# Attention and a gated FFN in one kernel: 128-query scores from halves of q and k, and the second pass's low halves of weights on VectorE

## The chip, the cores and the metric

The kernel runs on one core of one Trainium2 chip. The metric is the device time of one execution in microseconds. The kernel before takes 665.92 us, the median of three runs (665.81 to 666.36).

## The reference

Causal attention with 4 batches, 12 heads, 448 positions and a head size of 64, then an RMS norm over the 768 model columns and a gated FFN with 1536 hidden columns on all 1792 tokens, in fp32:

```python
scores = scale * np.matmul(q, k.transpose(0, 1, 3, 2))
scores = np.where(mask, -1000000000.0, scores)
scores = scores - np.max(scores, axis=-1, keepdims=True)
attn = np.exp(scores)
attn = attn / (np.sum(attn, axis=-1, keepdims=True) + 1e-09)
x = np.matmul(attn, v)            # then (tokens, 768)
rms = np.sqrt(np.mean(x * x, axis=-1, keepdims=True) + 1e-06)
xn = x / rms * rms_g
g = xn @ w_gate
silu = g * (1.0 / (1.0 + np.exp(-g)))
val = xn @ w_val
return silu * val @ w_out
```

## The kernel before

The tokens are cut into three groups. Groups 0 and 1 hold the first 256 queries of two batches each, group 2 the last 192 queries of all four. Attention is cut into 60 units; a unit is a pair of heads (64 rows of the array each) and a set of queries. Units 0 to 11 make group 0, 12 to 23 group 1 (256 queries each). Units 24 to 59 make group 2: in each six, four of 128 queries of one batch (kind 1) and two of 64 queries of two batches (kind 2). In order of their numbers, 24, 25 and 26 are kind 1, 27 and 28 kind 2, 29 to 32 kind 1, 33 and 34 kind 2, and so on.

The FFN multiplies in fp32r. Each operand is cut into a high half (`h`, a cast on ScalarE) and a low half (`l`, what is left, a subtraction on VectorE or GpSimd), and a product is three: high by high, high by low, low by high (L508 to L510 in the first two passes, L658 in the third). The scores (L195) are plain fp32 products of the loaded q and k, which hold both in one tile (`qk_r`): 128 columns of queries and 384 of keys for kind 1.

Three passes run over the FFN. While the first works on group 0, group 1's attention is made; while the second works on group 1, that of group 2. The third, for group 2, follows alone. In a pass a tick is two row blocks of one weight unit, six products of 128x512, then a step of the attention if one is due. Delayed work is posted to a later tick (`post`), and a table of delays (`T`) says how many ticks later; `tick()` then emits it at the end of that tick. The order on every engine is the order in which the code emits it.

In the second pass the attention goes in visits of two units, one visit about every four ticks (`round_of_two`). The visit of p makes the scores of units p + 3 and p + 4 and the products with v of p and p + 1. The scores stay in PSUM until VectorE masks them (L204), ScalarE takes the exponential (L207), VectorE the reciprocal of the sums (L216) and GpSimd multiplies by it (L212). In the next three ticks and at the start of the next visit the weights are transposed, one head a tick, into the single bank t (L251), which VectorE (L255) or ScalarE (L257) copies out.

The q and k of unit p + 4 are loaded two ticks after the scores of p, into one of four buffers (tag `qk`). All loads go through SyncE's queue in the order of the code. Weights are loaded too (`w_r`), cut into halves by `split_w`, and summed in place on VectorE (L483) for the third pass, after which four stores (`wy`, `wz`) write them out. In the second pass the low half of a weight unit (`w_l`) is made by GpSimd (L105, called from L466); in the first by VectorE (L464).

Of the kernel before, what the change touches and what calls it, by code (L numbers as in the profile page):

```python
# [11 lines left out]
F32R = mybir.dt.float32r  # L12
I32 = mybir.dt.int32
BF16 = mybir.dt.bfloat16
ALU = mybir.AluOpType
# [4 lines left out]
B, H, S, D = 4, 12, 448, 64  # L20
DM = H * D
DFF = 1536
P = 128
NP = H // 2
KD = DM // P
NF = DFF // P
NU = 2 * NF + 2 * KD
W = 512
# [9 lines left out]
for i in range(2 * 2 * NP, len(UNITS), NP):  # L38
    UNITS[i + 3: i + 6] = UNITS[i + 4: i + 6] + UNITS[i + 3: i + 4]
LAST = {(g, c): max(i for i, u in enumerate(UNITS) if u[0] == g and u[2] == c)  # L40
        for g in range(NG) for c in range(NP)}
ENDS = [max(i for i, u in enumerate(UNITS) if u[0] == g) + 1 for g in range(NG)]
MASKED = -8.0e9


# [19 lines left out]
def attention_ffn(ctx: ExitStack, tc: tile.TileContext, qk0, qk1, qk2, v, v2, w, g, out, out2):  # L65
# [7 lines left out]
    nc = tc.nc  # L73
# [17 lines left out]
    raw = pool("raw", 4, att, side="right")  # L91
# [9 lines left out]
    def f32(ap):  # L101
        return ap.bitcast(F32)
# [12 lines left out]
    for m, r, n in ((mask, 0, P), (mask2, 0, D), (mask2, D, D)):  # L115
        wd = m.shape[1]
# [17 lines left out]
    def post(delay, fn):  # L134
        if delay <= 0:
            fn()
        else:
            later.setdefault(now[0] + delay, []).append(fn)
# [11 lines left out]
    nsc = -1.0 / float(D) ** 0.5  # L150
    av_ps = bank("a").rearrange("p (s c) -> p s c", s=2)

    def load_qk(p):
        if p < len(UNITS):
            _, kind, _, _, row, _ = UNITS[p]
            raw_qk[p] = raw.tile([P, 2, W], F32, tag="qk", name="qk_r")
            if kind == 2:
                nc.sync.dma_start(out=raw_qk[p], in_=qk2[row])
            else:
                nc.sync.dma_start(out=raw_qk[p][:, 0], in_=(qk0, qk1)[kind][row])  # L160
# [14 lines left out]
    def steps_s(p):  # L175


        if not 0 <= p < len(UNITS):
            return []
        _, kind, _, _, _, _ = UNITS[p]  # L180
        pr = hs[p] = dict(norms=[])
        bl = blocks(kind)
        nb = 2 * len(bl)

        def scores(pss):
            for i, (o, wd) in enumerate(bl):
                for h in range(1 + (kind == 2)):
                    for e in range(2):
                        r = raw_qk[p][e * D: (e + 1) * D, h]
                        if kind == 2:  # L190
                            ps, q0, nq = pss[e][h * D: (h + 1) * D, :wd], 0, D
                        else:
                            ps, q0, nq = pss[e][:, o: o + wd], i * P, P
                        k0 = nq if kind else 2 * P
                        nc.tensor.matmul(ps, r[:, q0: q0 + nq], r[:, k0: k0 + wd],  # L195
                                         start=True, stop=True)

        def softmax(e, i, pss):
            o, wd = bl[i]
            ps, sp = pss[e][:, o: o + wd], pr["sp"][e][:, o: o + wd]  # L200
            n = len(bl) * e + i
            nm, sm, rs = (pr[m][:, n: n + 1] for m in ("nm", "sm", "rs"))
            mk = mask2 if kind == 2 else mask[:, 3 * P - wd:]
            nc.vector.tensor_tensor_reduce(  # L204
                out=sp, in0=ps, in1=mk, scale=nsc, scalar=3.0e38,
                op0=ALU.add, op1=ALU.min, accum_out=nm)
            post(T["exp" if p >= ENDS[0] else "exp0"], lambda: nc.scalar.activation(  # L207
                sp, sp, AF.Exp, bias=nm, scale=-1.0, accum_out=sm))
            if p == ENDS[0] - 1:
                pr["norms"].append(lambda: nc.scalar.mul(sp, sp, rs))  # L210
            else:
                pr["norms"].append(lambda: nc.gpsimd.tensor_scalar(  # L212
                    sp, sp, rs, 1.0, op0=ALU.mult, op1=ALU.mult))

        def norm():
            nc.vector.reciprocal(pr["rs"][:, :nb], pr["sm"][:, :nb])  # L216
            post(2 if p == ENDS[0] - 1 else 0, lambda: [f() for f in pr["norms"]])

        def step():
            for nm in ("nm", "sm", "rs"):  # L220
                pr[nm] = st_p.tile([P, 4], F32, tag=nm, name=nm)
            pr["sp"] = [sp_p.tile([P, S], F32, tag="sp", name="sp") for _ in range(2)]
            pss = [bank(t_) for t_ in "xy"] if p > ENDS[0] + DP and p % 2 == 0 else [
                bank("s", 2), bank("y") if p == ENDS[0] else bank("s", 2)]
            scores(pss)
            for e in range(2):
                for i in range(len(bl)):
                    softmax(e, i, pss)
            post(T["exp" if p >= ENDS[0] else "exp0"], lambda: nc.scalar.activation(
                pr["sm"][:, :nb], pr["sm"][:, :nb], AF.Identity, bias=tiny))  # L230
            post(T["norm1" if kind else "norm0" if p < ENDS[0] else "norm"], norm)
            post(2, lambda: load_qk(p + 4))

        return [step]

# [221 lines left out]
    def split_w(s):  # L457
        if s < 2 * NU:
# [1 line left out]
            h = ws_p.tile([P, DM], F32R, tag="wh", name="w_h")  # L460
            l = ws_p.tile([P, DM], F32R, tag="wl", name="w_l")
            nc.scalar.copy(h, t)  # L462
            if s < NU or s > NU + 2 * NF and s % 2:
                post(T[("wl0", "wl0", "wl2", "wl2", "wl4")[s] if s < 5 else "wl"], lambda: nc.vector.tensor_tensor(l, t, f32(h), op=ALU.subtract))  # L464
            else:
                post(T["wl"], lambda: pool_op(l, t, ALU.subtract, f32(h)))  # L466
# [402 lines left out]
    with tc.manual_schedule():  # L869
# [32 lines left out]
        n = 0  # L902
# [181 lines left out]
```

## Time and profile before

| | |
|---|---|
| median of three runs | 665.92 us |
| the profiled execution's own time | 667.3 us |
| its span | 665.5 us |
| TensorE busy (matmuls) | 657.1 us, 99% |
| TensorE weight loads | 552.8 us, 83% |
| VectorE | 494.5 us, 74% |
| ScalarE | 378.0 us, 57% |
| GpSimd | 290.6 us, 44% |
| granted TensorE clock | full speed in all slices |
| chain that ended last | 91% TensorE, 4% ScalarE, 2% VectorE, 1% GpSimd |

The shares are those of the whole span. The change lies in the second pass, from about 205 to 420 us, and what it is worth there is read from that stretch. A matmul's busy time overlaps that of the next one, so what a product costs in a row of products is read from the distance of their starts.

### The profile page before, as it was taken

The page shows a single profiled execution, that of the slowest core. Times are in us where ns is not written, and L with a number is a line of the kernel's source. Part 1 is how long each engine was busy: PE and PEld are TensorE (multiplying, and loading weights), DVE is VectorE, ACT ScalarE, POOL GpSimd, SP SyncE. Part 2 cuts the span into 40 slices and gives each one's busy share as a digit, 9 for nine tenths or more (in the row PEclk, how much of TensorE's full clock was granted, in tenths as well). Part 3 has the DMA queues.
Part 4 walks back from the last instruction along what each step waited for, and adds up shares of the span by engine and source line. Part 5 has one row for each costly group of instructions (what it writes and reads, how often), then busy time and mean ns, then how long its engine had stood idle before and what let it go on. Part 6 is the DMA issues. An engine that isn't in the chain of part 4 may idle for free.

```text
span 665.5 us, 11886 instructions
## 1 busy us (share of the span) xinstructions
PE 657.1 (99%) x4122; PEld 552.8 (83%) x4122; DVE 494.5 (74%) x1013; ACT 378.0 (57%) x837; POOL 290.6 (44%) x278
## 2 busy tenths in 40 slices
PE   9999999999999999999999999999999999999997
PEld 6667877778877777777777778888999999999997
DVE  5997987889876665677666874496776866889982
ACT  6996866767865546565656555334533444365540
POOL 4770313245444355766667575653424342401220
PEclk9999999999999999999999999999999999999999
DMA  8876898888796366866658455235766466473541
GB/s 256 292 257 217 246 288 268 263 280 255 241 335 238 119 200 197 277 199 234 221 199 268 157 195 175 83 114 189 239 221 234 127 229 209 155 218 92 154 143 60
DMA packets 71356, 138.81 MB, mean 209 GB/s; under 512 B 7744, under 2 KB 39232, under 8 KB 71296
## 3 DMA queue, kind: packets, MB, share of 16 engines
q1 hardware_dynamic: 71296, 138.05, 63.6%
q8 instruction: 33, 0.54, 0.3%
q14 instruction: 27, 0.22, 0.1%
HBM read 104.21 MB, written 33.82 MB: 207 GB/s over the span
## 4 chain that ended last, share of the span: by engine, by line
PE 91%; ACT 4%; DVE 2%; POOL 1%; issue 1%; DMA 0%; SPq 0%; DVEq 0%; ACTq 0%; POOLq 0%
PE m_ps L508 15%; PE m_ps L510 14%; PE m_ps L509 14%; PE s_ps L658 10%; PE m_ps L658 9%; PE a_ps L280 6%; PE y_ps L658 5%; PE t_ps L251 5%; PE x_ps L658 4%; PE s_ps L195 4%; PE x_ps L195 2%; ACT sp L207 2%; POOL sp L212 1%; PE m_ps L867 1%; DVE sp L204 1%
## 5 line engine op out<-in xcount | busy, mean ns | idle before, releaser
L212 POOL TENSOR_SCALAR sp<-sp,rs 128x384 f32<-128x384 f32 (+3 forms) x164 | 121.7, 759 | 165.6 <-DVE rs L216 142.3
L508 PE MATMUL m_ps<-xh,w_h 128*128 128x512 f32 x276 | 116.8, 423 | 0.0
L510 PE MATMUL m_ps<-xh,w_l 128*128 128x512 f32 x276 | 108.5, 393 | 0.0
L509 PE MATMUL m_ps<-xl,w_h 128*128 128x512 f32 x276 | 107.9, 391 | 0.0
L207 ACT ACTIVATE sp<-sp,nm 128x128 f32<-128x128 f32 (+3 forms) x168 | 87.1, 522 | 20.4 <-DVE nm L204 20.3
L105 POOL TENSOR_TENSOR a_l<-w_q,a_h 128x768 fp32r<-128x768 f32 x24 | 48.2, 2008 | 80.1 <-ACT a_h L549 78.7
L257 ACT COPY pt<-t_ps 128x384 f32<-128x384 f32 (+1 forms) x65 | 32.1, 493 | 52.5 <-PE t_ps L251 52.5
L510 PEld LDWEIGHTS m_ps<-xh,w_l 128*128 128x128 f32 x276 | 51.8, 188 | 11.7
L508 PEld LDWEIGHTS m_ps<-xh,w_h 128*128 128x128 f32 x276 | 51.9, 188 | 11.3 <-issue 3.3
L105 POOL TENSOR_TENSOR w_l<-w_r,w_h 128x768 fp32r<-128x768 f32 x30 | 57.3, 1913 | 6.7 <-ACT w_h L462 6.5
L204 DVE CUSTOM_DVE_ANT_0 sp<-s_ps,mask 128x128 f32<-128x128 f32 (+2 forms) x114 | 42.6, 423 | 23.3 <-PE s_ps L195 22.5
L509 PEld LDWEIGHTS m_ps<-xl,w_h 128*128 128x128 f32 x276 | 52.1, 189 | 8.1 <-issue 0.2
L508 PE MATMUL m_ps<-hh,w_h 128*128 128x512 f32 x144 | 58.1, 403 | 0.0
L251 PE MATMUL t_ps<-ident,sp 128*128 128x128 f32 (+1 forms) x348 | 56.4, 274 | 1.0 <-ACT pt L257 1.0
L251 PEld LDWEIGHTS t_ps<-ident,sp 128*128 128x128 f32 (+1 forms) x348 | 42.8, 138 | 17.2 <-POOL sp L212 3.1
L510 PE MATMUL m_ps<-hh,w_l 128*128 128x512 f32 x144 | 56.2, 391 | 0.0
L509 PE MATMUL m_ps<-hl,w_h 128*128 128x512 f32 x144 | 56.1, 390 | 0.0
L280 PEld LDWEIGHTS a_ps<-pt,v_r 128*64 128x64 f32 (+1 forms) x816 | 36.7, 137 | 18.6 <-issue 8.9
L280 PE MATMUL a_ps<-pt,v_r 112*64 112x64 f32 (+2 forms) x816 | 46.3, 262 | 0.9 <-DVE pt L255 0.8
L549 ACT CAST a_h<-w_q 128x768 fp32r<-128x768 f32 (+1 forms) x48 | 35.0, 754 | 14.1 <-DMA w_q<-wz 4.1
L255 DVE COPY pt<-t_ps 128x384 f32<-128x384 f32 (+1 forms) x43 | 25.3, 588 | 20.9 <-PE t_ps L251 20.8
L105 POOL TENSOR_TENSOR acc<-acc,sq 128x384 f32<-128x384 f32 (+1 forms) x19 | 23.4, 1235 | 36.5 <-ACT sq L346 33.7
(196 smaller groups left out, 1644.1 us busy)
## 6 DMA issues: line engine op xcount, KB each, us to landing
w<-in_w SPq DMA_DIRECT2D x36, 768.0 KB, 5.1
w<-w_c SPq DMA_DIRECT2D x36, 384.0 KB, 5.6
w_r<-w SPq DMA_DIRECT2D x36, 384.0 KB, 5.0
qk_r<-in_qk SPq DMA_DIRECT2D x48, 256.0 KB, 4.4
qk_r<-in_qk SPq DMA_DIRECT2D x12, 512.0 KB, 6.5
v_r<-in_v SPq DMA_DIRECT2D x12, 448.0 KB, 4.1
v_r<-in_v SPq DMA_DIRECT2D x24, 192.0 KB, 3.0
wy<-w_r SPq DMA_DIRECT2D x24, 192.0 KB, 4.3
```

The lines of the kernel that those rows point to most:

```text
L105: nc.gpsimd.tensor_tensor(out_, a, b, op=op)
L195: nc.tensor.matmul(ps, r[:, q0: q0 + nq], r[:, k0: k0 + wd], start=True, stop=True)
L204: nc.vector.tensor_tensor_reduce(out=sp, in0=ps, in1=mk, scale=nsc, scalar=3.0e38, op0=ALU.add, op1=ALU.min, accum_out=nm)
L207: post(T["exp" if p >= ENDS[0] else "exp0"], lambda: nc.scalar.activation(sp, sp, AF.Exp, bias=nm, scale=-1.0, accum_out=sm))
L212: pr["norms"].append(lambda: nc.gpsimd.tensor_scalar(sp, sp, rs, 1.0, op0=ALU.mult, op1=ALU.mult))
L251: nc.tensor.transpose(ps[:kb, at: at + P], pr["sp"][e][:, o + kb * j: o + kb * (j + 1)], ident)
L280: nc.tensor.matmul(at_[e * D: (e + 1) * D, p % 2, q0: q0 + n], raw_v[p][:kb, h, j, e, :], pr["pt", e][:kb, a0: a0 + n], start=(j == 0), st ...
L508: nc.tensor.matmul(ps, wh[:, k, :], mh, start=(first and k == ks[0]), stop=False)
L509: nc.tensor.matmul(ps, wh[:, k, :], ml, start=False, stop=False)
L510: nc.tensor.matmul(ps, wl[:, k, :], mh, start=False, stop=(last and k == 5))
L549: nc.scalar.copy(h, src)
L658: nc.tensor.matmul(ps, a[x], b[y], start=first and n == 0, stop=last and n == 2, skip_group_check=True)
```

## The change

For 23 of the 24 units of kind 1 (all but unit 24), q and k are cut into halves like an operand of the FFN: `halve_qk` casts the loaded 128x512 to a high half on ScalarE, and a tick later VectorE subtracts for the low half. The scores of such a unit are then three fp32r products a head (`scores_of_halves`) in place of one fp32 product. The halves take a buffer of tag `qk` for each unit; the raw q and k of two units share one. The halving is posted two ticks after the scores of the unit two before it (three ticks where that one's number is even), and from unit 21 on the loads of q and k are posted five ticks after the scores and not two. Besides, the 24 low halves of the second pass's gate and value weights go from GpSimd to VectorE.

```diff
+HALVED = ENDS[1] + 1
...
+    halves, halved = {}, {p for p, u in enumerate(UNITS) if p >= HALVED and u[1] == 1}
+
+    def halve_qk(p):
+
+        x = raw_qk[p - (p + 1) % 2][:, (p + 1) % 2]
+        t = halves[p] = raw.tile([P, 2, W], F32R, tag="qk", name="qk_h")
+        nc.scalar.copy(t[:, 0], x)
+        post(1, lambda: nc.vector.tensor_tensor(t[:, 1], x, f32(t[:, 0]), op=ALU.subtract))
+
     def load_qk(p):
         if p < len(UNITS):
             _, kind, _, _, row, _ = UNITS[p]
+            if p in halved and p % 2 == 0:
+                nc.sync.dma_start(out=raw_qk[p - 1][:, 1], in_=qk1[row])
+                return
...
+        def scores_of_halves(pss):
+            wd = bl[0][1]
+            for n, (a, b) in enumerate(((0, 0), (0, 1), (1, 0))):
+                for e in range(2):
+                    q, k = (halves[p][e * D: (e + 1) * D, i] for i in (a, b))
+                    nc.tensor.matmul(pss[e][:, :wd], q[:, :P], k[:, P: P + wd], start=n == 0, stop=n == 2)
...
-            scores(pss)
+            (scores_of_halves if p in halved else scores)(pss)
...
-            post(2, lambda: load_qk(p + 4))
+            if p + 2 in halved:
+                post(2 + (p + 1) % 2, lambda: halve_qk(p + 2))
+            post(5 if p >= HALVED - 4 else 2, lambda: load_qk(p + 4))
...
-            if s < NU or s > NU + 2 * NF and s % 2:
+            if s < NU + 2 * NF or s % 2:
```

The lines of the kernel after are 22 or so further on: L216 there is the product of halves, L161 the low half of q and k, L160 the cast, L277 the copy of transposed weights (L255 before), L505 the sum in place (L483), L486 w_l on VectorE (L464), L549 and L557 what L527 and L535 were, L224 the masking, L236 the reciprocal.

On TensorE, at the visit that scores units 37 and 38, before:

```order
L251 MATMUL t_ps<-ident,sp 128x128 x3
L195 MATMUL s_ps<-qk_r 128x384 x2
L195 MATMUL x_ps<-qk_r 128x384
L195 MATMUL y_ps<-qk_r 128x384
L280 MATMUL a_ps<-pt,v_r 64x64 x16
```

and after:

```order
L273 MATMUL t_ps<-ident,sp 128x128 x3
L216 MATMUL s_ps<-qk_h 128x384 x6
L216 MATMUL x_ps<-qk_h 128x384
L216 MATMUL y_ps<-qk_h 128x384
L216 MATMUL x_ps<-qk_h 128x384
L216 MATMUL y_ps<-qk_h 128x384
L216 MATMUL x_ps<-qk_h 128x384
L216 MATMUL y_ps<-qk_h 128x384
L302 MATMUL a_ps<-pt,v_r 64x64 x16
```

Four products have become twelve; what stands ahead and behind is the same.

On VectorE, between the two copies of transposed weights ahead of that visit and its masking, before:

```order
L255 COPY pt<-t_ps 112x512
L216 RECIPROCAL rs<-sm 128x2 x2
L527 SCALAR_TENSOR_TENSOR t_sb<-t_sb,gr 128x512
L483 TENSOR_TENSOR w_r<-w_r 128x384 x2
L535 TENSOR_TENSOR t_sb<-t_sb,m_ps 128x512
L255 COPY pt<-t_ps 128x384
L483 TENSOR_TENSOR w_r<-w_r 128x384
L204 ISA sp,nm<-s_ps,mask 128x384
```

and after:

```order
L277 COPY pt<-t_ps 112x512
L236 RECIPROCAL rs<-sm 128x2 x2
L549 SCALAR_TENSOR_TENSOR t_sb<-t_sb,gr 128x512
L505 TENSOR_TENSOR w_r<-w_r 128x384 x2
L486 TENSOR_TENSOR w_l<-w_r,w_h 128x768
L161 TENSOR_TENSOR qk_h<-qk_r,qk_h 128x512 x2
L557 TENSOR_TENSOR t_sb<-t_sb,m_ps 128x512
L277 COPY pt<-t_ps 128x384
L505 TENSOR_TENSOR w_r<-w_r 128x384
L224 ISA sp,nm<-s_ps,mask 128x384
```

A low half of weights and both low halves of q and k have come in between the two copies.

On SyncE's queue, around the loads of units 37 and 38 (the second `qk_r` row) and of 39 and 40 (the third), before:

```order
L160 DMA qk_r<-in_qk 128x512 x2
L433 DMA w_r<-w_4_130 128x768
L169 DMA v_r<-in_v 128x384
L167 DMA v_r<-in_v 112x1024
L160 DMA qk_r<-in_qk 128x512 x2
L487 DMA wy_163<-w_r 128x384 x2
L487 DMA wz_175<-w_r 128x384 x2
L433 DMA w_r<-w_16_142 128x768
L167 DMA v_r<-in_v 112x1024
L169 DMA v_r<-in_v 128x384
L158 DMA qk_r<-in_qk 128x1024 x2
```

and after:

```order
L455 DMA w_r<-w_4_130 128x768
L173 DMA qk_r<-in_qk 128x512
L167 DMA qk_r<-in_qk 128x512
L182 DMA v_r<-in_v 128x384
L180 DMA v_r<-in_v 112x1024
L509 DMA wy_163<-w_r 128x384 x2
L509 DMA wz_175<-w_r 128x384 x2
L455 DMA w_r<-w_16_142 128x768
L173 DMA qk_r<-in_qk 128x512
L167 DMA qk_r<-in_qk 128x512
L180 DMA v_r<-in_v 112x1024
L182 DMA v_r<-in_v 128x384
```

The loads of units 37 and 38 have moved behind the four stores and a load of weights.

## Rows read from the trace of the kernel before

**Rows 1.** Busy time by engine in a stretch: PE, PEld, DVE, ACT, POOL, clock, DMA.

```profile
216.00:420.00 204.00, 202.96 (x1603) 155.50 (x1602) 134.22 (x331) 115.34 (x273) 125.25 (x118) 1.00 0.61 201
```

**Rows 2.** TensorE's waits from 216 to 420 us: total, times, longest.

```profile
PE t_ps L251 <- ACT pt L257: 1.0, 3, 0.7
...
PEld t_ps L251 <- POOL sp L212: 2.2, 3, 1.1
```

**Rows 3.** Chain of waits around the visit at 282 us: start, duration, what.

```profile
281.80 0.33 PE t_ps L251 x3
282.12 0.85 PE s_ps L195 x4
282.97 0.32 PE x_ps L195
...
283.61 1.74 PE a_ps L280 x44
```

**Rows 4.** TensorE in order of time, scores of one unit (start, duration).

```profile
303.23 0.19 PEld L195 LDWEIGHTS x_ps<-qk_r 64*128 64x128 f32 x1
303.24 0.19 PEld L195 LDWEIGHTS y_ps<-qk_r 64*128 64x128 f32 x1
...
303.55 0.48 PE L195 MATMUL x_ps<-qk_r 64*128 64x384 f32 x1
...
303.56 0.48 PE L195 MATMUL y_ps<-qk_r 64*128 64x384 f32 x1
```

**Rows 5.** TensorE in order of time, third pass; 23 such products lie between.

```profile
479.82 0.34 PE L658 MATMUL s_ps<-cl,a_h 128*128 128x384 f32 x1
...
483.98 0.34 PE L658 MATMUL y_ps<-cl,a_h 128*128 128x384 f32 x1
```

**Rows 6.** Groups over the whole span: count, busy us, mean ns, idle before.

```profile
L483 DVE TENSOR_TENSOR w_r<-w_r 128x384 f32<-128x384 f32 x48 | 36.7, 782 | 0.0
L538 DVE TENSOR_TENSOR hl<-t_sb,hh 128x512 fp32r<-128x512 f32 x12 | 8.2, 681 | 0.0
...
L536 ACT CAST hh<-t_sb 128x512 fp32r<-128x512 f32 x24 | 14.8, 617 | 6.0 <-DVE t_sb L535 6.0
...
L105 POOL TENSOR_TENSOR w_l<-w_r,w_h 128x768 fp32r<-128x768 f32 x30 | 57.3, 1913 | 6.7 <-ACT w_h L462 6.5
```

**Rows 7.** Instructions of two lines: ns, shortest, median, longest; first and last start.

```profile
L483 DVE TENSOR_TENSOR w_r<-w_r x48: 534/550/2171, 231.4 to 412.2; 128x384 f32<-128x384 f32 x48
L464 DVE TENSOR_TENSOR w_l<-w_r,w_h x6: 916/947/2605, 406.1 to 454.6; 128x768 fp32r<-128x768 f32 x6
```

**Rows 8.** VectorE and GpSimd in order of time, near 292 us.

```profile
291.21 3.42 DVE L483 TENSOR_TENSOR w_r<-w_r 128x384 f32<-128x384 f32 x2
292.08 2.13 POOL L105 TENSOR_TENSOR w_l<-w_r,w_h 128x768 fp32r<-128x768 f32 x1
```

**Rows 9.** VectorE, GpSimd and TensorE in order of time, ahead of two visits.

```profile
268.45 0.69 DVE L255 COPY pt<-t_ps 112x512 f32<-112x512 f32 x1 [0.32 <-PE t_ps L251]
...
268.60 1.28 POOL L105 TENSOR_TENSOR hl<-t_sb,hh 128x512 fp32r<-128x512 f32 x1
...
270.17 0.92 PE L195 MATMUL s_ps<-qk_r 64*128 64x384 f32 x4
...
280.11 0.69 DVE L535 TENSOR_TENSOR t_sb<-t_sb,m_ps 128x512 f32<-128x512 f32 x1 [1.63 <-PE m_ps L510]
280.72 0.55 DVE L255 COPY pt<-t_ps 128x384 f32<-128x384 f32 x1
```

**Rows 10.** SyncE's issues in order of time; then issues by line, median us to landing.

```profile
262.33 0.91 SPq L160 DMA_DIRECT2D qk_r<-in_qk  x2
...
275.45 2.61 SPq L487 DMA_DIRECT2D wz<-w_r  x2
...
qk_r<-in_qk SPq DMA_DIRECT2D x48, 256.0 KB, 4.4
qk_r<-in_qk SPq DMA_DIRECT2D x12, 512.0 KB, 6.5
```

## The prediction

> **What bounds the kernel now.** I read the stretch table first, then the waits, the chain of waits, and the instructions by group. In the stretch from 216 to 420 us, where the second pass and the 128-query units run, TensorE is busy 202.96 of 204.00 us at a granted clock of 1.00, VectorE 134.22, ScalarE 115.34, GpSimd 125.25 [rows 1]. Busy TensorE is not TensorE at its peak, so I asked who releases it: its matmuls waited 1.0 us for the copies of transposed weights (L257), its weight loads 2.2 us for GpSimd's normalization (L212), three times each [rows 2]. So the stretch is a row of matmuls with a few small holes. A change is worth what it takes from that row, less what it puts in as holes; work on the other engines counts only where it comes late.
>
> **The scores on TensorE.** A visit scores two units. For a pair that the change halves, the chain goes from 282.12 to 283.61, 1.49 us [rows 3]. That is four fp32 passes of 0.32 us over 384 keys (two to a unit, both heads in each) and 0.21 us for getting in and out. The heads run side by side: x_ps and y_ps start at 303.55 and 303.56, their weight loads at 303.23 and 303.24 [rows 4]. The new form is three fp32r products to a unit and head, so six pairs of products in a visit. No row shows an fp32r product on half the rows of the array; the nearest is the FFN's with the same 384 columns on all rows, of which 24 take from 479.82 to 483.98, 0.173 us each [rows 5]. With the heads side by side the visit takes 6 x 0.173 + 0.21 = 1.25 us and saves 0.24. There are eleven such visits (units 25 and 26, 29 and 30, and so on to 55 and 56), and one of a single unit that saves half. Sum: 11.5 x 0.24 = **2.8 us saved**. Bounds: half of an fp32 pass, 0.160 a pair, would save 0.32 a visit, 3.7 us; 0.183 a pair (0.01 for the second head, as in [rows 4]) 0.18, 2.1 us.
>
> What speaks against side by side is that a pair now needs two weight loads in half the time. The two loads of a pair start 10 ns apart [rows 4], so there they don't take turns. The Trainium skill (TensorEngine Tiling (Array Packing), Key Properties) says the same of separate tiles: loads and products run in parallel. Another of its pages (TensorE: Matmul & The Clock Gate, LDWEIGHTS) gives a load's time by its columns alone, columns / 1.2 ns, whatever the rows; were the two loads of a pair to take turns at that 0.107 us, an estimate from this page, a pair would take 0.21 and the visit 1.49: nothing saved.
>
> **VectorE and GpSimd.** GpSimd loses 24 low halves of weights of 1.91 us [rows 6], 46 of its 125 us. VectorE gains them at 0.95 us, the median of the six that it makes already [rows 7], 22.7 us, and 23 low halves of q and k of 128x512. For these the nearest row is the hidden layer's low half of the same size and kind, 0.68 us [rows 6]: 15.7 us. ScalarE gains 23 casts at 0.62 us [rows 6], 14 us on 115 of 204. VectorE would go from 134 to 173 of 204 us, were nothing given back. Something is: its in-place sums (L483), all but a few in this stretch, take 0.55 us by the median and 0.78 on the mean [rows 6, 7], 48 x 0.23 = 11 us more than they need. One cause: two of them take 3.42 us, to 294.63, while GpSimd runs w_l until 294.21 [rows 8]. The Trainium skill (SBUF — State Buffer, on the shared port pair) has this as an exclusive lock between a VectorE instruction with two SBUF inputs and a GpSimd one that reads SBUF; the trace agrees. It cuts both ways: w_l leaves GpSimd, but the 47 new VectorE instructions are of the kind that is held up.
>
> So the question is not VectorE's sum but its queue. TensorE wants two things of it in time. First, the copy of the transposed weights (L255), since bank t is single. I set the work added between two of these copies against VectorE's idle time there. Ahead of the visit at 282 a w_l and both low halves come in, 0.95 + 2 x 0.68 = 2.31 us, where it idled 1.63; so the copy that began at 280.72 comes 0.68 us later, ends at 281.95, and the transposes wanted the bank at 281.80 [rows 3, 9]: a wait of 0.15, and more if GpSimd holds one of the three up. I take 0.5. Two more stretches are built like this with less excess; 0.3 each. Second, the new wait: the scores wait for the low halves, and behind them on TensorE stand the products with v and the FFN. Ahead of the visit at 270 VectorE goes: copy at 268.45 (0.69), w_l 0.95, low half 0.68, done at 270.77. The second unit's scores would start at about 270.17 + 0.21 + 3 x 0.173 = 270.90, so just in time; but hl on GpSimd runs from 268.60 to 269.88 [rows 9], w_l starts behind it, and the low half ends at 271.5: a wait of 0.6 us, of which I take 0.5, since GpSimd's order may shift. At most other visits the second low half stands without a w_l behind the copy. Added holes: 0.5 + 0.3 + 0.3 + 0.5 = **1.6 us**; bounds 0 and, at 0.5 for each of the eleven visits, 5.5.
>
> Back comes part of the old holes, since the transposed weights come through VectorE's sums and GpSimd's normalization, and w_l no longer stands among these. Of the 2.2 us [rows 2] I take **0.8**; bounds 0 and 2.2.
>
> **The loads.** On SyncE's queue the q and k loads go three ticks later, behind a w_r load and the four stores of sums, which wait for VectorE. That of units 37 and 38 was issued at 262.33 [rows 10]; it now follows the stores and a w_r, about 4 us later, at 266, and lands some 4.4 us after that, at 271. ScalarE's cast of it comes two ticks after the visit at 270, about 274. The loads of 512 KB (units 39 and 40) go behind stores that end at 278.06, and the second waits for the low half of unit 38, which frees its buffer, to about 281; with 6.5 us [rows 10] they land by 288, and the visit is at 292. What queues behind on SyncE, the v loads, waits for the visit at 282 in any case. So I cost this at nothing. Without that cover a 512 KB load would stall TensorE by some 2 us at each of six visits.
>
> **Sum.** -2.8 + 1.6 - 0.8 = -2.0 us. The profiled execution took 667.3 us, 665.5 of span and 1.8 around it, so it would take 665.3; it is 1.4 above the median of 665.92. From the median: **663.9 us**.
>
> **Rivals.** (1) *VectorE eats the gain.* The same mechanism as above at more places: the holes come to 2.3 to 4.9 us instead of 1.6, and the time stays between 664.6 and 667.2. For it: VectorE at 80 to 85%. Against: it idled 70 of 204 us. (2) *The second unit's low half is late at every visit*, by one held-up instruction. The break-even is 2.8 / 11 = 0.25 us a visit. At 0.64 us, half of hl [rows 9], it is 11 x 0.64 - 2.8 = +4.2: **670.1**, slower. Against it: at most visits nothing but one short sum stands between the copy and that low half. (3) *The two heads take turns*, in products or loads. Then a visit takes at most 12 x 0.173 + 0.21 = 2.29, 0.80 more than now: 11.5 x 0.80 = +9.2, **675.1**. The page on weight loads stands for a milder form. Against it: [rows 4]. (4) *More comes back*: 0.160 a pair, no added holes, half of the old ones gone: 3.7 + 1.1, **661.1**.
>
> **How the numbers follow.** Faster or slower by over 0.2% (1.3 us) is about what a measurement of this kernel can tell from no change. Forecast, between 661.5 and 664.6: 0.53; (4) 0.05; (1) 0.25; (2) 0.12; (3) 0.05. Faster 0.58, same 0.25, slower 0.17. The range takes in the forecast and (1) whole: 661.5 to 667.5. It leaves out (3), most of (2), and most of (4).
>
> **What would show it.** A visit's scores (L216) at 1.25 us in the chain; 1.17 or 1.31 would be the bounds, 1.5 or 2.3 rival (3). New waits of TensorE for L161 below 2 us in sum, the largest at the visit near 270; 5 us or more would be (2). In-place sums (now L505) near 0.6 us on the mean. GpSimd near 79 us in the stretch, VectorE near 165. Wrong from the ground would be TensorE waiting for a q and k load, or more than before for GpSimd.

## The result and the profile after

The change made the kernel slower: 669.82 us median (669.16 to 671.06, six runs) against 666.14 us (665.79 to 667.25, six runs); ratio 1.0054, 95% interval 1.0044 to 1.0064. Forecast were 663.9 us and a range of 661.5 to 667.5. The profiled execution of the changed kernel took 669.83 us, its span 668.1.

The stretch table of the kernel after, 216 to 420 us (columns as in [rows 1]):

```profile
216.00:420.00 204.00, 199.41 (x1627) 155.10 (x1625) 162.37 (x373) 124.20 (x289) 102.81 (x90) 1.00 0.61 200
```

Against [rows 1] TensorE is busy 3.6 us less, though the clock is 1.00 in both. VectorE came out as forecast (162 for 165), GpSimd did not (103 for 79). TensorE's waits from 200 to 425 us, after (total, times, longest; PE are its matmuls, PEld its weight loads):

```profile
PE t_ps L273 <- DVE pt L277: 1.3, 3, 0.6
PE x_ps L216 <- DVE qk_h L161: 1.3, 2, 0.6
...
PE t_ps L273 <- POOL sp L232: 0.9, 3, 0.4
...
PEld t_ps L273 <- POOL sp L232: 3.9, 6, 0.9
...
PEld x_ps L216 <- DVE qk_h L161: 2.1, 3, 1.0
```

The wait for GpSimd's normalization, 2.2 us in [rows 2], did not shrink but grew to 3.9, and the matmuls' own wait for it, 0.9, is new. New too are 1.3 and 2.1 us for the low halves (L161) and 1.3 for VectorE's copies (L277). A matmul's wait and that of its weight load fall into the same time, so they must not be added. The chain at the visit at 282 us, after, beside [rows 3] (start, duration, what):

```profile
282.75 0.72 PE s_ps L216 x6
283.47 0.17 PE x_ps L216
...
283.65 0.17 PE x_ps L216
...
283.82 0.17 PE x_ps L216
...
284.00 1.02 PE a_ps L302 x29
```

From 282.75 to 284.00 are 1.25 us where there were 1.49: the scores save just what was forecast. The groups of the four instructions in question, after, 205 to 402 us (count, busy us, mean ns, idle before):

```profile
L232 POOL TENSOR_SCALAR sp<-sp,rs 128x384 f32<-128x384 f32 x44 | 38.4, 889 | 65.7 <-DVE rs L236 52.8 <-PE t_ps L273 12.9
L232 POOL TENSOR_SCALAR sp<-sp,rs 128x448 f32<-128x448 f32 x23 | 32.6, 1432 | 36.5 <-DVE rs L236 33.0 <-PE t_ps L273 3.5
L505 DVE TENSOR_TENSOR w_r<-w_r 128x384 f32<-128x384 f32 x43 | 26.4, 633 | 0.0
L486 DVE TENSOR_TENSOR w_l<-w_r,w_h 128x768 fp32r<-128x768 f32 x24 | 24.3, 1013 | 0.0
L161 DVE TENSOR_TENSOR qk_h<-qk_r,qk_h 128x512 fp32r<-128x512 f32 x21 | 18.8, 897 | 0.0
```

The same normalization took in the kernel before:

```profile
L212 POOL TENSOR_SCALAR sp<-sp,rs 128x384 f32<-128x384 f32 x44 | 29.1, 678 | 58.7 <-DVE rs L216 48.2 <-PE t_ps L251 10.5
L212 POOL TENSOR_SCALAR sp<-sp,rs 128x448 f32<-128x448 f32 x24 | 20.1, 856 | 17.4 <-DVE rs L216 17.4
```

So the in-place sums (782 to 633 ns on the mean, [rows 6]) gained what was hoped, but GpSimd's normalization, which the change does not touch, went from 0.68 to 0.89 and from 0.86 to 1.43 us, and the low half takes 0.90 us instead of 0.68. Where this stops TensorE is seen first at the visit at 348.5 us. VectorE in order of time, after (start, duration):

```profile
346.94 0.56 DVE L277 COPY pt<-t_ps 128x384 f32<-128x384 f32 x1 [0.26 <-PE t_ps L273]
347.41 1.00 DVE L486 TENSOR_TENSOR w_l<-w_r,w_h 128x768 fp32r<-128x768 f32 x1
348.34 1.76 DVE L161 TENSOR_TENSOR qk_h<-qk_r,qk_h 128x512 fp32r<-128x512 f32 x1
350.03 0.55 DVE L224 CUSTOM_DVE_ANT_0 sp<-s_ps,mask 128x384 f32<-128x384 f32 x1
```

and GpSimd and TensorE there:

```profile
347.65 1.90 POOL L106 TENSOR_TENSOR hl<-t_sb,hh 128x512 fp32r<-128x512 f32 x1
```

```profile
350.16 0.44 PE L216 MATMUL x_ps<-qk_h 64*128 64x384 f32 x1 [0.64 <-DVE qk_h L161]
```

The low half takes 1.76 us beside hl on GpSimd. The visit's second unit starts on time, at 349.18, since its first pair of products reads the high halves alone. The second pair reads the low half and was due 0.17 us later; it starts at 350.16, some 0.8 us late.

The same happens to w_l ahead of the visit at 304.29 before. VectorE, GpSimd and TensorE, after:

```profile
294.13 2.02 DVE L486 TENSOR_TENSOR w_l<-w_r,w_h 128x768 fp32r<-128x768 f32 x1
```

```profile
293.75 1.58 POOL L106 TENSOR_TENSOR hl<-t_sb,hh 128x512 fp32r<-128x512 f32 x1
```

```profile
299.93 0.52 PE L273 MATMUL t_ps<-ident,sp 128*128 128x128 f32 x3 [0.65 <-DVE pt L277]
```

Beside hl this w_l takes 2.02 us, 1.01 on the mean. Four maskings and the copy of transposed weights stand behind it on VectorE, and the transposes wait 0.65 us for that copy.

In the other kind of hole GpSimd is held. VectorE and GpSimd near 312 us, after:

```profile
312.22 0.94 DVE L486 TENSOR_TENSOR w_l<-w_r,w_h 128x768 fp32r<-128x768 f32 x1
313.07 0.68 DVE L161 TENSOR_TENSOR qk_h<-qk_r,qk_h 128x512 fp32r<-128x512 f32 x1
```

```profile
312.43 1.69 POOL L232 TENSOR_SCALAR sp<-sp,rs 128x384 f32<-128x384 f32 x1 [6.22 <-PE t_ps L273]
```

A normalization that takes 0.58 us at its shortest takes 1.69 while VectorE runs two instructions with two SBUF inputs, and the weight load of the transposes at 314.18 waits 0.9 us for it.

To see where the 6 us go I took from each trace the start of the first product with v of a visit, and its difference to the kernel before, both set to zero at the visit at 186.59 us. The last five columns are experiments below.

| visit, before | after | no low halves, no w_l | low half from PSUM | w_l loaded | no low halves | both from PSUM |
|---|---|---|---|---|---|---|
| 250.58 | +0.48 | -0.60 | -0.19 | -0.09 | -0.69 | -0.22 |
| 294.00 | +0.71 | -1.03 | -0.44 | -0.44 | -1.06 | +0.27 |
| 304.29 | +2.04 | -1.29 | +0.89 | -0.69 | +0.24 | -0.02 |
| 314.82 | +3.09 | -1.08 | +1.07 | -0.91 | +0.24 | +0.02 |
| 336.91 | +2.87 | -1.30 | +0.85 | -1.11 | +0.04 | -0.20 |
| 347.43 | +3.55 | -1.53 | +0.62 | -1.34 | -0.19 | -0.43 |
| 369.50 | +3.32 | -1.75 | +0.39 | -1.56 | -0.41 | -0.65 |
| 380.02 | +4.35 | -1.98 | +0.16 | -1.32 | -0.64 | -0.55 |
| 400.94 | +3.96 | -2.52 | -0.20 | -1.87 | -1.04 | -1.07 |

Where nothing is late a visit takes back 0.22 to 0.26 us (336.91, 369.50). The loss comes at a few places: 294 to 304 (+1.3), 304 to 315 (+1.1), 347 (+0.7) and 380 (+1.0). The first is that of the w_l at 294.13, and it is as large without low halves of q and k (-1.06 to +0.24). The other three are gone without low halves and, but for half a microsecond at 380, with w_l loaded and so not made.

### The profile page after: what moved, and what is told of

Read it like the earlier page. It is cut to its first block, busy times and chain, and to the rows that moved or that the text cites. A ratio compares the mean times of both kernels' runs of the same rounds, so it can differ in the third digit from the quotient of the medians.

```text
span 668.1 us, 12029 instructions
## 1 busy us (share of the span) xinstructions
PE 655.6 (98%) x4168; PEld 554.2 (83%) x4168; DVE 524.1 (78%) x1060; ACT 389.8 (58%) x860; POOL 271.8 (41%) x254
## 4 chain that ended last, share of the span: by engine, by line
PE 82%; DVE 6%; ACT 6%; issue 3%; POOL 2%; DMA 1%; SPq 0%; DVEq 0%; POOLq 0%; ACTq 0%
PE m_ps L530 13%; PE m_ps L532 12%; PE m_ps L531 12%; PE s_ps L680 10%; PE m_ps L680 9%; PE a_ps L302 6%; PE y_ps L680 5%; PE x_ps L680 4%; PE t_ps L273 4%; ACT sp L227 2%; PE s_ps L208 2%; POOL sp L232 2%; DVE qk_h L161 1%; PE x_ps L208 1%; PE s_ps L216 1%
## 5 line engine op out<-in xcount | busy, mean ns | idle before, releaser
L232 POOL TENSOR_SCALAR sp<-sp,rs 128x384 f32<-128x384 f32 (+3 forms) x164 | 146.0, 907 | 191.8 <-DVE rs L236 162.6
L224 DVE CUSTOM_DVE_ANT_0 sp<-s_ps,mask 128x128 f32<-128x128 f32 (+2 forms) x114 | 42.7, 423 | 17.9 <-PE s_ps L208 13.0
L474 DVE SCALAR_TENSOR_TENSOR w_c<-w_c,w 128x768 int32<-128x768 int32 x36 | 35.9, 998 | 1.9
L486 DVE TENSOR_TENSOR w_l<-w_c,w_h 128x768 fp32r<-128x768 f32 x36 | 37.0, 1027 | 0.6 <-ACT w_h L484 0.5
```

The lines of the kernel that those rows point to most:

```text
L224: nc.vector.tensor_tensor_reduce(out=sp, in0=ps, in1=mk, scale=nsc, scalar=3.0e38, op0=ALU.add, op1=ALU.min, accum_out=nm)
L232: pr["norms"].append(lambda: nc.gpsimd.tensor_scalar(sp, sp, rs, 1.0, op0=ALU.mult, op1=ALU.mult))
L474: (at3, lambda: nc.vector.scalar_tensor_tensor(out=ti, in0=ti, scalar=3, in1=lo, op0=ALU.logical_shift_left, op1=ALU.bitwise_or)),
```

## Experiments: which part

Theory A is VectorE's queue, too long by what was added. Theory B is a lock: VectorE's instructions with two SBUF inputs and GpSimd's, which read SBUF, hold each other up. Theory C blames the low halves of q and k alone. Diffs are against the kernel after unless said; ratios are to the kernel before, run on the same chip.

**w_l back on GpSimd.**

```
-            if s < NU + 2 * NF or s % 2:
+            if s < NU or s > NU + 2 * NF and s % 2:
```

> The changed kernel with the low halves of the second pass's gate and value weights (w_l) back on GpSimd; the scores of halves and the low halves of q and k on VectorE stay. Theory A (VectorE's queue: what was added ahead of its copies and low halves makes them late, by its length alone): VectorE loses 24 x 0.95 = 23 of its 162 us in the stretch 216 to 420, the holes shrink by more than half, and the time is 2.8 us below the kernel before plus 1 to 2 us of holes, about 664 to 665. Theory B (the lock: VectorE's instructions with two SBUF inputs and GpSimd's normalization hold each other up): GpSimd gets 24 x 1.91 us of the same kind back, every low half of q and k can now fall under one of them, and the time stays at 669 or goes up to 671. Theory C (the low halves of q and k alone are the cause, whoever makes w_l): 668 to 670.

670.38 us, ratio 1.0062 (1.0043 to 1.0081): no better than the change. VectorE is at 147.29 us in the stretch, not 162, and nothing is won, against A. The time is the same whichever of the two engines makes w_l, but the places differ: the largest loss in this trace, 3.0 us between 369.50 and 380.02, is where GpSimd makes w_l and hl and VectorE's sum and low half beside them take 2.07 and 1.74 us.

**w_l moved, nothing else** (against the kernel before; the same line the other way).

> The kernel before with one part of the change: VectorE makes w_l of the second pass, not GpSimd. The scores stay in fp32, so nothing is saved on TensorE. Theory A: VectorE goes from 134 to about 155 us in the stretch, some copies of transposed weights come late, 0.5 to 1 us each at a third of the eleven visits: 667 to 669. Theory B: w_l is of the locked kind either way, and GpSimd has 46 us less of it, so the normalization comes earlier or as before: 665 to 666.5. Theory C: 665 to 666.5, as B.

667.60 us, 1.0017 (1.0008 to 1.0026). The move by itself costs some 1 us, as A expected; the normalization of 128x384 went from 0.68 to 0.81 us all the same, which B had as unchanged or better. In the trace all of it (+1.1) stands between 294.00 and 304.29, where w_l takes 2.02 us beside hl, as in the change: a hold-up of VectorE by GpSimd, which B had not counted.

**No low halves of q and k.**

```
-        post(1, lambda: nc.vector.tensor_tensor(t[:, 1], x, f32(t[:, 0]), op=ALU.subtract))
...
-                    q, k = (halves[p][e * D: (e + 1) * D, i] for i in (a, b))
+                    q, k = (halves[p][e * D: (e + 1) * D, i] for i in (0, 0))
```

> The changed kernel without the low halves of q and k: they are not made, and the three products of each head all read the high halves, so the low part of the scores is left out and TensorE's work is the same. VectorE loses 23 x 0.9 = 21 us. Theory A: the new waits for L161 go (about 3.4 us in the trace of the changed kernel), and a part of the late copies: 664 to 666. Theory B: 664 to 666 too, with GpSimd's normalization of 128x384 back from 0.89 towards 0.70 us. Theory C: all of the loss goes, 662.5 to 664. Should the loss sit in the later loads or in w_l instead, it stays at 668 or more.

665.28 us, 0.9981 (0.9972 to 0.9989): in the range of both A and B, with the normalization of 128x384 back at 0.81 us. C wanted more.

**No w_l.**

```
-            l = ws_p.tile([P, DM], F32R, tag="wl", name="w_l")
+            l = h if NU <= s < NU + 2 * NF else ws_p.tile([P, DM], F32R, tag="wl", name="w_l")
...
-            if s < NU + 2 * NF or s % 2:
+            if l is h:
+                pass
+            elif s < NU or s % 2:
```

> The changed kernel with no w_l made for the gate and value weights of the second pass by any engine; the products that read it read the high half, so the low part of these weights is left out and TensorE's work is the same. VectorE loses 24 x 1.0 = 24 us, GpSimd gains nothing. Theory A: as with w_l on GpSimd, 663.5 to 665. Theory B: the lock is left with the low halves of q and k and the in-place sums only; the normalization comes back half way, 664.5 to 666.5, and, unlike under A, it is clearly below the kernel with w_l on GpSimd (by 3 us or more). Theory C: 667 to 669.

664.60 us, 0.9972 (0.9962 to 0.9982). That is 5.8 us below the kernel with w_l on GpSimd, the gap that B asked for; C falls.

**Neither** (both diffs).

> The changed kernel with neither the low halves of q and k nor the second pass's w_l made; the products that read them read the high halves, so both low parts are left out and TensorE's work is the same. Each of the two alone brought the time down from 669.8 to about 665. If the two losses add up (each makes its own holes), taking both away gives about 661; if either one alone is harmless and only both together overfill VectorE, it gives no more than the better of the two, 664 to 664.6. The first is what the lock (B) wants, since w_l and the low halves each meet GpSimd's normalization alone; the second is the queue (A).

663.65 us, 0.9960 (0.9948 to 0.9973). The two losses don't add up as I wrote for B (about 661); the result is nearer to what I wrote for A (664 to 664.6). From here the low halves alone cost 1.0 us (664.60), w_l alone 1.6 (665.28), both 6.2 (669.82). What has to be explained is the 3.6 us that only the two together cost; a lock can do that too, where two held-up instructions meet, so the next runs ask for queue or lock directly.

**The kernel before without w_l** (the same edit there).

> The kernel before without the second pass's w_l of gate and value weights (the products read the high half, so the low part of these weights is left out; TensorE's work is the same, the scores stay in fp32). It prices the new scores: without w_l and low halves the halved kernel took 663.65, 2.5 us less than the kernel before. If that is the scores' 2.8 us alone, w_l costs the kernel before next to nothing and this run takes 666 to 666.5. If a part of it is w_l leaving GpSimd (I had put 0.8 us on the old holes), it takes 665 to 665.5, and the scores saved 1.5 to 2 us.

666.05 us, 0.9991 (0.9981 to 1.0001): w_l costs the kernel before 0.6 us, hardly to be told from nothing. The scores, with the casts and the later loads, thus saved 0.9991 - 0.9960 of 666, 2.1 us net.

## Experiments: queue or lock

**Low half with one operand from PSUM.**

```
-        post(1, lambda: nc.vector.tensor_tensor(t[:, 1], x, f32(t[:, 0]), op=ALU.subtract))
+        post(1, lambda: nc.vector.tensor_tensor(
+            t[:, 1], av_ps.rearrange("p s c -> p (s c)"), x, op=ALU.subtract))
```

> The changed kernel with one operand of the low halves of q and k exchanged: the subtraction reads bank a in PSUM and the raw q and k, not the raw ones and their high half. It is as long (other 128x512 instructions with one PSUM input took 0.68 to 0.69 us, the low half alone 0.68), stands at the same place in VectorE's queue, but has one SBUF input instead of two. The low half has wrong values, so the low part of the scores is not computed; TensorE's work is the same. Theory A (queue): nothing changes, 669 to 670. Theory B (lock between VectorE's two SBUF inputs and GpSimd): the low half goes from 0.90 to 0.69 us on the mean, GpSimd's normalization of 128x448 from 1.43 to about 0.9, and the time comes to that of the kernel without low halves, 665 to 667.

665.97 us, 0.9998 (0.9989 to 1.0007), what B expected: 3.9 of the 6.2 us gone, though VectorE makes as many instructions in the same order. The line in this run, 205 to 402 us, as a group and then with shortest, median and longest ns:

```profile
L161 DVE TENSOR_TENSOR qk_h<-a_ps,qk_r 128x512 fp32r<-128x512 f32 x21 | 14.2, 680 | 0.0
L233 POOL TENSOR_SCALAR sp<-sp,rs 128x448 f32<-128x448 f32 x24 | 20.7, 881 | 37.1 <-DVE rs L237 33.6 <-PE t_ps L274 3.5
```

```profile
L161 DVE TENSOR_TENSOR qk_h<-a_ps,qk_r x21: 674/680/686, 235.1 to 396.0; 128x512 fp32r<-128x512 f32 x21
```

In the kernel after the same view says:

```profile
L161 DVE TENSOR_TENSOR qk_h<-qk_r,qk_h x21: 676/684/1776, 235.5 to 400.2; 128x512 fp32r<-128x512 f32 x21
```

With one SBUF input no low half is held up any more, three of them beside hl included, and the 128x448 normalization is at 0.88 us, not 1.43. The same visit as above (348.5 after), in this run:

```profile
345.38 0.95 DVE L487 TENSOR_TENSOR w_l<-w_r,w_h 128x768 fp32r<-128x768 f32 x1
346.25 0.68 DVE L161 TENSOR_TENSOR qk_h<-a_ps,qk_r 128x512 fp32r<-128x512 f32 x1
347.46 0.56 DVE L225 CUSTOM_DVE_ANT_0 sp<-s_ps,mask 128x384 f32<-128x384 f32 x1 [0.53 <-PE s_ps L217]
```

VectorE now waits 0.53 us for the scores instead of TensorE for it. The Trainium skill (SBUF — State Buffer, Who interferes with whom) says that a VectorE instruction with at most one SBUF input, "outside the 2-port perf modes", does not contend with GpSimd; here all 21 agree, at 674 to 686 ns.

**The same with right values.** ScalarE copies q and k into PSUM bank x or y, idle between visits.

```
+        c = bank("xy"[(p + 1) % 2])
+        nc.scalar.copy(c, x)
...
-        post(1, lambda: nc.vector.tensor_tensor(t[:, 1], x, f32(t[:, 0]), op=ALU.subtract))
+        post(1, lambda: nc.vector.tensor_tensor(t[:, 1], c, f32(t[:, 0]), op=ALU.subtract))
```

> The changed kernel, computing all of it, with the low halves of q and k made from a copy in PSUM bank x or y and their high half: one SBUF input instead of two, at the price of 23 copies of about 0.6 us on ScalarE. The lock (B) expects what the run with bank a as the operand gave, 666.0, plus 0 to 1 us for ScalarE's copies ahead of its exponentials: 666 to 667.5, with low halves of 0.68 us each and GpSimd's normalization of 128x448 at 0.9. The queue (A) expects 669 to 671.

667.44 us, 1.0011 (1.0001 to 1.0022), in what B expected: 2.4 us below the change, low halves at 0.68, the normalization of 128x448 at 0.91 us.

**w_l with one operand from PSUM**, low halves as in the change (bank a read twice, 384 columns each).

```
+            a, b = (x.rearrange("p (s c) -> p s c", s=2) for x in (l, t))
+            c = av_ps.rearrange("p s c -> p (s c)")[:, :HX].unsqueeze(1).broadcast_to([P, 2, HX])
+            nc.vector.tensor_tensor(a, c, b, op=ALU.subtract)
```

> The changed kernel with one operand exchanged in w_l of the second pass alone: it reads bank a in PSUM in place of one SBUF input; the low halves of q and k stay as in the change. w_l has wrong values, so the low part of these weights is not computed; TensorE's work is the same. B: as without w_l, 664.6 to 665.2, GpSimd's normalization of 128x448 back from 1.43 to about 1.0 us. A: 667 to 670, since VectorE's queue is as long as in the changed kernel.

666.62 us, 1.0006 (0.9998 to 1.0015): 3.2 us gone with VectorE at 161.66 us in the stretch, as full as in the change. It is not all of the 5.2 that leaving w_l out gave; between the two numbers expected. The normalization of 128x448 came back to 1.00 us, as B said.

**Both from PSUM.**

> The changed kernel with one operand exchanged in both of VectorE's new instructions: the low halves of q and k and w_l read bank a in PSUM in place of one of their two SBUF inputs. Both keep their place and length in VectorE's queue. Their values are wrong, so the low parts of the scores and of these weights are not computed; TensorE's work is the same. If all that is left of the loss (2.3 us between the run with the low half from PSUM, 665.97, and the run with neither, 663.65) is w_l's lock (B), this takes 663.6 to 664.3, VectorE being as full as in the changed kernel. If it is w_l's 23 us in VectorE's queue (A), it stays at 665.6 to 666.2.

665.63 us, 0.9983 (0.9974 to 0.9992), at the low end of what A expected. With the low halves out of the lock, taking w_l out of it brings 0.3 us more by the medians, 1.0 by the ratios, where it brought 3.2 with them in. Its groups, 205 to 402 us, show the lock gone but for the sums and hl:

```profile
L233 POOL TENSOR_SCALAR sp<-sp,rs 128x384 f32<-128x384 f32 x44 | 29.3, 684 | 82.0 <-DVE rs L237 67.6 <-PE t_ps L274 14.5
L233 POOL TENSOR_SCALAR sp<-sp,rs 128x448 f32<-128x448 f32 x24 | 19.0, 812 | 39.6 <-DVE rs L237 39.6
```

The w_l that took 2.02 us beside hl in the change is no longer held, though hl runs beside it here too (293.59 to 295.17):

```profile
293.96 0.94 DVE L484 TENSOR_TENSOR w_l<-a_ps,w_r 128x768 fp32r<-128x768 f32 x1
```

But the exchange brings a wait of its own, since the products with v write the bank that w_l now reads: those at 294.96 wait for the end of this w_l (TensorE's waits, 205 to 402 us):

```profile
PEld a_ps L303 <- DVE w_l L484: 1.4, 1, 1.4
```

So of the 6.2 us the second SBUF inputs cost 4.2 by the medians (669.82 - 665.63) and 4.7 by the ratios (1.0054 - 0.9983), with as many instructions on VectorE (158 us busy for 162). What is left to the run with neither, 2.0 or 1.5 us, is VectorE's queue and that one new wait. In the traces it is 1.5 us (-1.07 against -2.52), and 0.7 of them come between 283.54 and 294.00, where that wait is.

## Experiments: the work moved elsewhere

**Low halves on GpSimd.**

```
-        post(1, lambda: nc.vector.tensor_tensor(t[:, 1], x, f32(t[:, 0]), op=ALU.subtract))
+        post(1, lambda: pool_op(t[:, 1], x, ALU.subtract, f32(t[:, 0])))
```

> The changed kernel with the low halves of q and k made by GpSimd, w_l by VectorE. VectorE loses 19 us, GpSimd gains 23 x 1.4 = 32 us and would be busy for 125 of 204 us. Theory A: VectorE's queue is as short as without low halves, but GpSimd's is longer, and the scores and transposes wait for it: 666 to 668.5. Theory B: the low halves stay two-input instructions of GpSimd, twice as long there, and now hold up w_l and the sums on VectorE and stand ahead of the normalization in one queue: 668.5 to 672.

684.50 us, 1.0272 (1.0257 to 1.0287), far worse than either theory expected. The granted clock was 0.994 to 0.997 in these runs, 0.999 to 1.000 in those of the change; at most some 4 us of it, an estimate from these shares, can be that. TensorE's waits, 200 to 425 us:

```profile
PEld x_ps L216 <- POOL qk_h L106: 8.0, 9, 1.2
PEld s_ps L216 <- POOL qk_h L106: 7.5, 7, 2.0
...
PE s_ps L216 <- POOL qk_h L106: 5.7, 7, 1.8
```

Both units' scores wait, at most visits: this is what my rival (2) looks like, with the low halves on the other engine. The low half takes 1.46 us there and stands behind up to four normalizations.

**Normalization on ScalarE** for the 128-query units.

```
-            if p == ENDS[0] - 1:
+            if p == ENDS[0] - 1 or p >= HALVED and kind == 1:
...
-            post(2 if p == ENDS[0] - 1 else 0, lambda: [f() for f in pr["norms"]])
+            post(2 if p == ENDS[0] - 1 else 1 if p >= HALVED and kind == 1 else 0, lambda: [f() for f in pr["norms"]])
```

> The changed kernel with the normalization of the 128-query units of the halved stretch on ScalarE (one tick later), not on GpSimd: 44 instructions of 0.6 us leave the lock, and ScalarE goes from 124 to about 151 of 204 us. VectorE's instructions stay as they are. Theory A: VectorE's copies and low halves come as late as before, and ScalarE's copies of transposed weights come later too: 669 to 672. Theory B: half of GpSimd's work that meets VectorE's two-input instructions is gone, the in-place sums, w_l and low halves get shorter (low half 0.75 us on the mean), and the transposes no longer wait for GpSimd at these units: 666 to 669.

671.70 us, 1.0079 (1.0067 to 1.0092). That is in the range of A. The low half came down to 0.74 us as B said (w_l did not, 1.04), but the time did not follow: the normalization is late on ScalarE instead (TensorE's waits, 200 to 425 us).

```profile
PEld t_ps L273 <- ACT sp L230: 7.1, 9, 1.5
...
PE t_ps L273 <- ACT sp L230: 3.1, 5, 1.0
```

**Half of w_l, then all, stored by the first pass and loaded by the second** (below: all; half has `if s % 2` in place of `if True`).

```
+    wl32 = {unit(s): dram.tile([P, DM], F32, name=f"wl32_{unit(s)}") for s in range(NU, NU + 2 * NF) if True}
...
+            if s < NU and s in wl32:
+                post(d + 2, lambda: nc.sync.dma_start(out=wl32[s], in_=f32(l)))
+            if NU <= s < NU + 2 * NF and unit(s) in wl32:
+                nc.sync.dma_start(out=f32(l), in_=wl32[unit(s)])
+            elif s < NU + 2 * NF or s % 2:
...
```

> The changed kernel, computing all of it, with every second low half of the second pass's gate and value weights not made again: the first pass stores it (12 stores of 384 KB on SyncE's queue), the second loads it. VectorE loses 12 x 1.0 us in the stretch. The lock (B) expects half of what the kernel without any w_l gained over the changed one: 667 to 668. If the holes come only where a w_l, a low half and a normalization meet, and the order decides which, it may be anywhere from 664.6 to 669. The price is in the first pass, where the DMA engines are at 0.81 and would go to about 0.88: should the stores hold back the loads of weights on SyncE, the time before 216 us grows and the gain is lost.

668.24 us, 1.0030 (1.0019 to 1.0041), just above what B expected: a third of the gain with half of the w_l gone.

> The changed kernel, computing all of it, with all 24 low halves w_l of the second pass stored by the first pass and loaded again, and the low halves of q and k as in the change (two SBUF inputs, VectorE). The stores cost the first pass nothing in the run that had them all, so this should behave as the kernel without any w_l: 664.6 to 665.5, faster than both kernels. If the 24 loads of 384 KB in the stretch (DMA engines from 0.61 to about 0.74) hold back loads of q, k, v or weights, 666 or more.

665.19 us, 0.9987 (0.9975 to 0.9998): computing everything, it beats the change by 4.6 us and the kernel before by 0.1%, little more than can be told. The DMA engines are at 0.90 of the first 216 us and 0.75 of the stretch (0.81 and 0.61 in the change), and from the visit at 103 us to that at 187 its visits keep their distance to those of the kernel before (0.53 and 0.55 us).

**All loaded, and low halves from banks x and y.**

> The changed kernel, computing all of it, with both causes taken away: all 24 w_l are stored by the first pass and loaded by the second, and the low halves of q and k are made from a copy of q and k in a PSUM bank (x or y, which idle between two visits; ScalarE makes the copy, 23 x 0.6 us) and their high half, so with one SBUF input. By the lock (B) the stretch should be as without w_l and low halves, 663.7 plus a little for ScalarE: 664 to 665, faster than both kernels. By the queue (A) the low halves still cost what they did without w_l, about 1 us: 664.6 to 666. If the 24 stores overfill the DMA engines in the first pass (0.81 to 0.95), that pass grows by some us, and the sum is 667 or more.

666.86 us, 1.0002 (0.9992 to 1.0013), above what A and B expected and not the best of both: with w_l gone the lock on the low halves is worth less than the 23 copies on ScalarE. The stores are not the reason, the first pass keeps its time here too. Its trace loses 0.8 us between the visits at 187 and 207, as the run with the copies alone does (the change: 0.35). In both, TensorE waits 0.8 us there for ScalarE's copy of transposed weights, ahead of which ScalarE has the copy of q and k to PSUM (0.58 us) and the cast.

## Why the prediction was wrong

**Scores: right.** 1.25 us a visit, as written; rival (3) is out, and the loads of a pair run side by side. The row of visits shows 0.22 to 0.26 us a visit, and net 2.1 us came out where 2.8 were counted.

**VectorE's sum and the in-place sums: right** (162 for 165; 0.63 for 0.6 us).

**Added holes: the step that failed.** 1.6 us were forecast, 6.2 found (from 663.65), above my bound of 5.5. I named the lock, wrote that it cuts both ways, and then worked with instructions of their own length: GpSimd's hold on VectorE got a price at two visits, 0.5 us at 270 and a part of the 0.5 at 282, and VectorE's hold on GpSimd got none. The traces put 6.5 us between the change and the run with neither (+3.96 and -2.52), 4.6 of them at four visits. At 304.29 it is 1.6 us, w_l held by hl; at 314.82 0.8, the normalization held and copies late; at 347.43 0.9, a low half held by hl; at 380.02 1.3, a normalization held (1.70 us) and then a low half by hl (1.78). At 270, where I had put 0.5, the trace shows only 0.1 more than a plain visit (1.38 for 1.25): the low half was not held there, and I had let the whole second unit wait for it, though its first pair reads high halves alone.

**GpSimd: priced at nothing.** What these 47 do to GpSimd stood in no term; I took GpSimd as 46 us lighter and so earlier. In fact its 67 normalizations went up from 49.2 (68 of them) to 71.0 us, so it lost 22 us instead of 46, and the transposes waited for it longer than before, which I had named as a sign of being wrong from the ground. The rows for it were there. [rows 8] shows VectorE held by GpSimd; the normalizations of the same trace, 205 to 402 us (ns, shortest, median, longest), would have shown the reverse:

```profile
L212 POOL TENSOR_SCALAR sp<-sp,rs x68: 578/588/2074, 211.6 to 398.3; 128x384 f32<-128x384 f32 x44, 128x448 f32<-128x448 f32 x24
```

The one of 2074 ns runs beside two of VectorE's in-place sums. After:

```profile
L232 POOL TENSOR_SCALAR sp<-sp,rs x67: 577/639/3839, 211.7 to 400.7; 128x384 f32<-128x384 f32 x44, 128x448 f32<-128x448 f32 x23
```

**Old holes given back: not far off.** Without w_l on any engine the kernel before gains 0.6 us where I had 0.8, though its interval reaches to no gain, and TensorE's waits for GpSimd come to 1.8 us there instead of 2.2. That moving w_l costs about 1 us is again an added hole, the w_l held by hl at 294.

**Rivals.** Rival (2), at 670.1, is nearest in number to the 669.82, and that is luck: its mechanism, one held-up low half, is there, but at two of eleven visits, at 348.5 and 382, where hl on GpSimd runs beside the second low half. The waits for L161, 2.1 us of weight loads with 1.3 of matmuls in the same time, are about the 2 that I had set as a limit, not the 5 of rival (2). Rival (1), more late places on VectorE, is nearest to what happened, with a price too small by over 2 us and the wrong cause: the length of the queue explains at most 2.0 of the 6.2 us.

**Loads: right.** The runs without low halves and w_l have the same late loads and still save 2.5 us; no score waited for a q and k load in the trace after. One wait of 0.7 us is put down to such a load, but it is a weight load for products with v, which do not read it, and the visits there (357.90 and 369.50) lose nothing.

**Not settled:** what VectorE's queue costs by its length alone (under 1 us in the traces, up to 2.0 by the medians), and why held-up instructions make a hole at some visits and none at others. The 3.6 us that w_l and low halves cost only together lie mostly at 314.82, 347.43 and 380.02. That both meet one normalization, as near 312 us, or one low half behind w_l meets hl, as at 348.5, fits the traces; no run moved one such instruction by itself.

## What to carry to other kernels

When work moves between VectorE and GpSimd, price what the moved instruction does to the other engine's queue as well as what is done to it, at every place where the two run side by side: count its SBUF inputs, and look which instructions on either side stand ahead of a matmul. An engine may come out relieved in the sum and still be later where it counts. Work that sits between two such engines is better taken away (here: stored once and loaded again, on DMA engines that had room) than moved; a PSUM operand takes it out of the lock, if the copy costs nothing.

## What the runs showed of the hardware

A GpSimd normalization of 128x448 that takes 0.64 us alone took up to 3.84 us in the kernel after while VectorE ran five instructions with two SBUF inputs beside it. One of 2.65 us (from 302.94) stayed held though VectorE's copy from PSUM (303.43, 0.68 us) left some 0.5 us between two of them, so GpSimd did not get in at the first gap (spans of GpSimd are rough). A VectorE subtraction of 128x512 took 0.68 us with one PSUM operand in every one of 21 cases, as long as with two SBUF operands undisturbed; the PSUM operand cost no time here. And the low half of 1.76 us (348.34 to 350.10) beside hl (347.65 to 349.55) means that VectorE stood for some 1.1 us, to near the end of GpSimd's instruction.
